# Thirty tiny loads on SyncE's DMA queue, in a decode step of attention beside an MLP

## The chip, the cores and the metric

The kernel runs on one core of a Trainium2 chip. The metric is the device time of one launch in microseconds (us), the median of several runs. Beside the plain runs there is one profiled execution, whose trace gives the times of single instructions and transfers.

## What is computed

```python
x = A_x                                   # 8 tokens (one for each sequence), 640 features
xn = layernorm(x)
q = (xn @ wq) -> 32 heads of 128          # per sequence
p = softmax(q . k_cache * 128**-0.5)      # k_cache, v_cache: [8, 32, 4096, 128], bf16
A = (p . v_cache -> 4096 features) @ wo   # wo: [4096, 640]
B = gelu(layernorm(xn) @ w1 + b1) @ w2 + b2   # 640 -> 1728 -> 640
out = x + A + B                           # [8, 1, 640] bf16
```

The K and V caches are 268 MB each; all the weights together are 15 MB. Each cache element is used once, with one query.

## The kernel before

**Tiles.** The 256 pairs of sequence and head are cut into 32 tiles of one sequence and eight heads. A K tile or a V tile is 8 MiB: 128 partitions (eight heads by 16 parts of the keys), each with 256 keys of 128 bf16 numbers, so 64 KB from one contiguous run of HBM for each partition. SBUF has three slots of that size: KA and KB take the K tiles in turn, VS takes every V tile. Outside the cache loop the same slots hold the weights: wq, q and w1 in VS, w2, b1, b2, x and small scratch in KB, wo in KA.

**Work on a tile.** `dve_chunk` (L701) lets VectorE multiply 176 of the 256 keys of each partition by the query, add and reduce, in two chunks; the other 80 are transposed on TensorE, copied by ScalarE and multiplied on TensorE (`scores`, L680). `act_exp` (L745) turns the tile's scores into probabilities, and `pe_PV` (L765) multiplies them with the V tile in 256 matmuls.

**Loads.** All large loads go out on SyncE's queue in one order. A load is made by the helpers `load` (L419), `load_w2` (L426), `load_k` (L432), `load_v` (L443), `load_wl` (L457) and `load_wn` (L465). Each records a `dma_start` and, ahead of it, the waits on what must be free: a K tile waits until VectorE is done with the K tile two before (the first one in KB waits for `pe_acc0`, L619), a V tile until the PV before has read VS. x and b1 go out on ScalarE's queue.

**The order.** Nothing runs while the helpers are called. `at(pos, fn, ...)` (L416) puts a call in a list, which is sorted by `pos` (L977); each engine records its calls, and the records are played at the end, SyncE's by one plain replay (L980). All instructions are issued by one line of the replay helper, which is why the profile gives line 218 for nearly everything. On SyncE the order before the cache loop is w1, w2 in two pieces, b2 (position -879), wq (-878, L893), the first K tile (-870, L894). Tile i has its work at about 100 i, so the last tile's V stands at 3150. V_CUT (L305) cuts that last V tile into three pieces of 4096, 2816 and 1280 KB. wo is loaded in five pieces: two ahead of the last V tile (2560 and 1280 KB, by WL_CUT) and three behind it (640, 480 and 160 KB, by WN_CUT = (24, 28, 31, 32), positions 3251 to 3253, L953).

**The end.** `fin_wn` (L844) multiplies each of the last three pieces of wo as it arrives into the accumulator that holds x, B and the other heads; `fin_store` (L854) copies, transposes and stores the result. SyncE's last act is to wait for that store.

Of the kernel before, what the change touches and what calls it, by code (L numbers as in the profile page):

```python
# [235 lines left out]
def _replay_pe(e, calls, head, mid, end, late, parity):  # L236

    n = len(head) - 1
    scores = [calls[a:b] for a, b in zip(head[:-1], mid)]
    values = [calls[a:b] for a, b in zip(mid[1:], head[2:] + [end])]  # L240
    assert mid[0] == head[1] and n & (n - 1) == 0

    def special(e, call, r):
        if call[0] != "wait_ge":
            return False
        for k, x in enumerate(parity):
            if x is call[1][0]:
                e.wait_ge(x, ((r + 2 - k) >> 1) * 16 + k)
                return True
        for x in late:  # L250
            if x is call[1][0]:
                e.wait_ge(x, ((r + n - 1) >> n.bit_length()) * 16 + 1)
                return True
        return False

    _replay(e, calls[:head[0]])
    with e.bass.Fori(0, n + 2, engines=OrderedEngineSet([e.engine])) as r:
        reg = e.to_reg(r)
        with e.If_ne(reg, 1):
            _play(e, values, r, 2, special)  # L260
        with e.If_lt(reg, n):
            _play(e, scores, r, 0, special)
        with e.If_eq(reg, n):
            _replay(e, calls[head[n]:mid[n]])
    _replay(e, calls[end:])


def bass_parallel_sum__gqa_block_cached__mixer_channel_mlp__decode_kernel(
# [32 lines left out]
    SLOT = NKEY * DH  # L301
    KA, KB, VS = 0, 1, 2
# [12 lines left out]
    def kslot(i):  # L315
        return KA if i % 2 == 0 else KB
# [4 lines left out]
    with ExitStack() as es:  # L321
        sb = lambda name, shape, dt: es.enter_context(nc.sbuf_tensor(name, shape, dt))
        ps = lambda name, shape, dt: es.enter_context(nc.psum_tensor(name, shape, dt))
        sem = lambda name: es.enter_context(nc.semaphore(name))
# [5 lines left out]
        def part(slot, lo, n, rows=P):  # L330
            return S_sb[0:rows, slot, lo:lo + n]
# [10 lines left out]
        def scratch(n, rows=P):  # L342
            ap = part(KB, o_[0], n, rows)
            o_[0] += n + n % 2
            return ap
# [11 lines left out]
        hT_sb = scratch(NF * B).rearrange("p (c b) -> p c b", b=B)  # L357
        iota_i = scratch(2 * P).bitcast(I32)
        ones_sb = scratch(B, 1)
        assert o_[0] <= SLOT  # L360

        KT_sb = sb("KT_sb", [P, 2, TPB, P], BF)
# [42 lines left out]
        pe, dve, act, sp, pool = (_Eng(sem(f"{n}_s")) for n in ("pe", "dve", "act", "sp", "pool"))  # L405
        pe2, act2 = _Eng(sem("pe2_s")), _Eng(sem("act2_s"))
        ld_s = [_Dma(sem(f"ld_s{s}")) for s in range(3)]
        ld_x, ld_b1, ld_b2, ld_wq, ld_w1, ld_w2, st_o = (
            _Dma(sem(n)) for n in ("ld_x", "ld_b1", "ld_b2", "ld_wq", "ld_w1", "ld_w2", "st_o"))
        ld_vl = [_Dma(sem(f"ld_vl{q}")) for q in range(1, len(V_CUT) - 1)]  # L410
        ld_wl = [_Dma(sem(f"ld_wl{q}")) for q in range(len(WL_CUT) - 1)]
        ld_wn = [_Dma(sem(f"ld_wn{q}")) for q in range(len(WN_CUT) - 1)]
        tk = {}
        prog = []

        def at(pos, fn, *a):  # L416
            prog.append((pos, len(prog), fn, a))
# [4 lines left out]
        def cache_src(cache, i):  # L422
            hq, b = divmod(i, B)
            return cache[b, hq * HS:(hq + 1) * HS].rearrange("h (p j) d -> (h p) j d", j=NKEY)
# [7 lines left out]
        def load_k(i):  # L432
            s = kslot(i)
            if i >= 2:
                sp.wait(tk[("km", i - 2)])
            elif s == KB:
                sp.wait(tk["acc"])
                ld_s[s].n += 1
            tk[("k", i)] = ld_s[s].sig(sp.dma_start(tile[s], cache_src(A_k_cache, i)))
            tk[("kk", i)] = [(ld_s[x].sem, (i + 2 - x) // 2 * 16 + x) for x in (KA, KB)]  # L440
            assert tk[("k", i)] == tk[("kk", i)][s]
# [23 lines left out]
        def load_wn(q):  # L465
            lo, hi = WN_CUT[q], WN_CUT[q + 1]
            tk[("wn", q)] = ld_wn[q].sig(sp.dma_start(
                woN_sb[:, lo - NL * HS:hi - NL * HS, :],
                A_wo[lo * DH:hi * DH, :].rearrange("(h p) n -> p h n", p=P)))

        def consts_pool():
            tk["iota"] = pool.sig(pool.iota(iota_i, [[1, P]], base=0, channel_multiplier=-1))
            for ap, v, d, k in (
                    (w2_sb[:, FR * D:], 0.0, ld_s[KB], 1), (ones_sb, 1.0, ld_vl[0], 1), (eps_sb[:, :], LN_EPS, ld_vl[1], 1),
                    (ini_sb[:, :], 0.0, ld_s[VS], 48), (rs_sb[:, :], 1.0, None, 0)):
                inst = pool.memset(ap, v)
                if d is not None:
                    inst.call[3] = (d.sem, k)
            assert len(ld_vl) == 2
            tk["consts"] = pool.sig(pool.memset(ones_f[:, :], 1.0))  # L480
# [409 lines left out]
        at(-879, load, "b2", ld_b2, b2_sb, B_b2.rearrange("(o f) -> o f", o=1))  # L890
        at(-890, load, "w1", ld_w1, w1_sb, B_w1.rearrange("(p c) f -> p c f", c=DC))
        at(-880, load_w2)
        at(-878, load, "wq", ld_wq, wq_sb, A_wq.rearrange("(p c) n -> p c n", c=DC))  # L893
        at(-870, load_k, 0)  # L894
        at(-800, consts_pool)
        at(-795, idents)
# [22 lines left out]
        for i in range(NQ):  # L919
            o = i * Q  # L920
            last = i == NQ - 1
            if i:
                at(o - 51, load_k, i)
            at(o + 50, load_v, i)
            at(o + 45, qrep, i + 1)
            at(o + 46, pe_qbc, i + 1)
            at(o + 46, act_qbc, i + 1)
            at(o, scores, i)
            at(o + 2, dve_chunk, i, 0)
            at(o + 52, dve_sel, i, 0)  # L930
            at(o + 55, dve_sel, i, 1)
            at(o + 58, dve_chunk, i, 1)
            at(o + 84, dve_max, i)
            at(o + Q + 45, act_exp, i)
            at(o + Q + 48, pe_RS, i)
            at(o + Q + 57, dve_rinv, i)
            at(o + Q + 50, pe_PV, i)
            if not last:
                at(o + Q + 71, act_O, i)
            at(o + Q + 75, o_norm, i)  # L940
# [7 lines left out]
        o = NQ * Q  # L948
        for q in range(len(WL_CUT) - 1):
            at(o - 55 + 0.1 * q, load_wl, q)  # L950
            at(o + 10 + q, fin_wl, q)
        for q in range(len(WN_CUT) - 1):
            at(o + 51 + q, load_wn, q)  # L953
            at(o + 80 + q, fin_wn, q)
# [28 lines left out]
        with nc.allow_low_precision(reason="each sum to bf16 has one bf16 term that is not masked to zero"):  # L983
            _replay_loop(nc.vector, dve.calls, marks["dve"])
        _replay_pe(nc.tensor, pe.calls, head, mid, end[0], [d.sem for d in ld_vl],
                   [ld_s[KA].sem, ld_s[KB].sem])
        nc.sync.wait_ge(*tk["out"])


# [26 lines left out]
```

## Time and profile before

| | us |
|---|---|
| median of 3 runs | 1282.88 (1282.83 to 1282.95) |
| the profiled execution | 1284.83 |
| its span, from the first instruction to the last | 1283.0 |

Of the span PE (TensorE) is busy 54%, VectorE 85%, ScalarE 37%, GpSimd 6%.

How to read the lines. A row of a timeline is: start in us from the span's start, length in us, engine (a q behind the name: the engine's instruction queue issues it), line, operation, output<-input, how often, and in brackets the engine's idle time ahead of it with what ended it. A row of the chain of waits is start, length, what. A row by window is: stretch, its length, then busy time and count of PE, PEld (weight loads), DVE (VectorE), ACT (ScalarE) and POOL (GpSimd), the granted TensorE clock, the busy share of the 16 DMA engines, and GB/s. A row of DMA issues ends in KB and us from issue to the landing of the last part; a row of one tensor gives the issue's shortest, median and longest length in ns, and the first and last start. A row of the queues gives packets, MB and share of 16 engines' time.

### The profile page before, as it was taken

How to read it: one execution, taken by the hardware profiler on the slowest of the kernel's cores; microseconds unless marked ns; L12 is line 12 of the kernel's file. 1: busy time of each engine (PE TensorE's matmuls, PEld its weight loads, DVE VectorE, ACT ScalarE, POOL GpSimd, SP SyncE). 2: the span in 40 equal slices, each digit the busy share in tenths (PEclk: the TensorE clock that was granted, in tenths of full speed). 3: DMA queues.
4: the chain of work that ended last, by engine and by line, in shares of the span. 5: the costliest groups of instructions: out<-in, count | busy, mean ns of one | idle time of the engine just before them, and what ended most of it. 6: DMA issues, size and time to landing. Idle time of an engine off the chain costs nothing.

```text
span 1283.0 us, 34713 instructions
## 1 busy us (share of the span) xinstructions
PE 697.1 (54%) x14014; PEld 581.1 (45%) x14014; DVE 1084.8 (85%) x574; ACT 474.2 (37%) x913; POOL 79.7 (6%) x79
## 2 busy tenths in 40 slices
PE   6856544564544664544664544654545654545655
PEld 2545443453443553433553434543434543434545
DVE  1699998988888988888988888988889988889884
ACT  2254322444322444323444223444223444223441
POOL 2013110000000000000000000000000000000001
PEclk8666555556555665656566656566556656555655
DMA  9999999999999999999999999999999999999998
GB/s 400 450 420 409 425 445 437 425 425 450 433 425 425 456 427 425 425 458 425 425 425 456 427 425 431 450 427 425 441 441 425 425 445 437 425 425 454 429 413 372
DMA packets 11584, 551.93 MB, mean 430 GB/s; under 512 B 1261, under 2 KB 2358, under 8 KB 2359
## 3 DMA queue, kind: packets, MB, share of 16 engines
q1 hardware_dynamic: 11506, 551.79, 99.6%
q8 instruction: 6, 0.10, 0.0%
q10 hardware_dynamic: 68, 0.02, 0.0%
q14 instruction: 4, 0.02, 0.0%
HBM read 551.80 MB, written 0.01 MB: 430 GB/s over the span
## 4 chain that ended last, share of the span: by engine, by line
DMA 76%; PE 21%; DVE 1%; issue 1%; POOL 0%; ACT 0%; SPq 0%; DVEq 0%; POOLq 0%
DMA S_sb<-in_A_v_cache_dram 71%; PE PV_ps L218 17%; PE TR_ps L218 2%; DMA S_sb<-in_A_k_cache_dram 2%; DMA S_sb<-in_A_wo_dram 2%; PE S_ps L218 1%; DMA S_sb<-in_B_w_dram 1%; DVE S_sb L218 1%; POOL qrep_sb L218 0%; PE QB_ps L218 0%; DVE ini_sb L218 0%; ACT KT_sb L218 0%; PE CH_ps L218 0%; PE ACC_ps L218 0%; SPq L218 0%
## 5 line engine op out<-in xcount | busy, mean ns | idle before, releaser
L218 PE MATMUL TR_ps<-ident_bf,S_sb 128*128 128x128 bf16 (+1 forms) x2570 | 340.2, 270 | 386.6 <-DMA S_sb<-in_A_k_cache_dram 358.7
L218 ACT ACTIVATE KT_sb<-TR_ps 128x1024 bf16<-128x1024 bf16 x320 | 327.6, 1024 | 459.2 <-PE TR_ps L218 447.3
L218 DVE TENSOR_TENSOR S_sb<-S_sb,qbc_sb 128x14976 bf16<-128x14976 bf16 x64 | 383.9, 5999 | 130.8 <-DMA S_sb<-in_A_k_cache_dram 129.5
L218 PEld LDWEIGHTS TR_ps<-ident_bf,S_sb 128*128 (+1 forms) x2570 | 243.6, 101 | 444.1 <-issue 387.5
L218 DVE TENSOR_REDUCE ini_sb<-S_sb 128x117 f32<-128x7488 bf16 x64 | 385.3, 6020 | 2.2
L218 PE MATMUL PV_ps<-P_sb,S_sb 128*128 128x8 bf16 x8448 | 231.3, 175 | 41.8 <-DMA S_sb<-in_A_v_cache_dram 39.3
L218 PEld LDWEIGHTS PV_ps<-P_sb,S_sb 128*128 128x128 bf16 x8448 | 228.8, 103 | 44.8 <-DMA S_sb<-in_A_v_cache_dram 42.1
L218 DVE TENSOR_TENSOR S_sb<-S_sb 128x7488 bf16<-128x7488 bf16 x64 | 197.9, 3091 | 2.2
L218 PE MATMUL S_ps<-qrep_sb,KT_sb 128*128 128x8 bf16 x2560 | 121.7, 177 | 29.8 <-ACT KT_sb L218 25.1
L218 ACT ACTIVATE P_sb<-ini_sb 128x256 bf16 (+1 forms) x256 | 126.0, 496 | 7.4 <-DVE ini_sb L218 7.4
L218 PEld LDWEIGHTS S_ps<-qrep_sb,KT_sb 128*128 128x128 bf16 x2560 | 90.9, 101 | 58.6 <-ACT KT_sb L218 40.6
L218 ACT ACTIVATE oU_sb<-PV_ps 128x8 f32<-128x8 f32 x32 | 5.7, 178 | 287.2 <-PE PV_ps L218 253.9
L218 POOL TENSOR_TENSOR oT_sb<-oU_sb,ri_sb 128x8 bf16<-128x8 f32 x31 | 52.1, 1680 | 391.9 <-ACT oU_sb L218 391.9
L218 POOL COPY qrep_sb<-qT_sb 128x128 bf16<-128x128 bf16 x33 | 19.0, 576 | 781.6 <-PE S_ps L218 751.2
L218 PE MATMUL CH_ps<-rs_sb,ones_f 128*128 128x8 f32 x66 | 19.5, 369 | 87.1 <-ACT P_sb L218 85.1
L218 PEld LDWEIGHTS CH_ps<-rs_sb,ones_f 128*128 128x128 f32 x66 | 16.5, 311 | 92.4 <-issue 92.4
L218 ACT ACTIVATION_READ_ACCUMULATOR P_sb<-ini_sb 128x1 f32 x256 | 48.5, 189 | 0.0
L218 DVE TENSOR_TENSOR S_ps<-S_ps,mask_sb 128x512 f32<-128x512 f32 (+1 forms) x65 | 32.5, 500 | 1.5 <-PE S_ps L218 1.5
L218 DVE TENSOR_REDUCE ini_sb<-S_ps 128x64 f32<-128x512 f32 x64 | 31.4, 491 | 2.2
L218 PE MATMUL QB_ps<-ident_bf,qrep_sb 128*128 128x128 bf16 x33 | 8.8, 268 | 23.5 <-POOL qrep_sb L218 23.1
L218 PEld LDWEIGHTS QB_ps<-ident_bf,qrep_sb 128*128 128x128 bf16 x33 | 3.3, 101 | 26.7 <-POOL qrep_sb L218 26.2
L218 DVE TENSOR_REDUCE ini_sb<-ini_sb 128x1 f32<-128x256 f32 x32 | 13.4, 420 | 1.1
(75 smaller groups left out, 135.3 us busy)
## 6 DMA issues: line engine op xcount, KB each, us to landing
S_sb<-in_A_wq_dram SPq DMA_DIRECT2D x1, 5120.0 KB, 24.0
S_sb<-in_A_v_cache_dram SPq DMA_DIRECT2D x1, 4096.0 KB, 15.3
S_sb<-in_A_v_cache_dram SPq DMA_DIRECT2D x1, 2816.0 KB, 18.6
S_sb<-in_A_wo_dram SPq DMA_DIRECT2D x1, 2560.0 KB, 31.8
S_sb<-in_B_w_dram SPq DMA_DIRECT2D x1, 2160.0 KB, 9.1
S_sb<-in_B_w_dram SPq DMA_DIRECT2D x1, 2080.0 KB, 12.1
S_sb<-in_A_wo_dram SPq DMA_DIRECT2D x1, 1280.0 KB, 34.5
S_sb<-in_A_v_cache_dram SPq DMA_DIRECT2D x1, 1280.0 KB, 21.3
```

What stands on the lines that cost most here:

```text
L218: inst = getattr(e, name)(*out, **kw)
```

## The change

A new helper, `ladder`, issues fifteen DMAs on SyncE's queue. The k-th of them, for k from 1 to 15, reads k runs of two bf16 numbers (4 bytes), 128 bytes apart, from b1 in HBM, and writes them into a scratch row of partition 0. Nothing reads them. They share one semaphore. The helper is called twice: at position -878.5, between b2 and wq, and at 3250.9, between the last piece of the last V tile and the first of the three last pieces of wo. The second K tile, whose slot holds the first scratch row, waits for the first fifteen loads; SyncE waits for all thirty before its wait for the store.

```diff
+        lad_sb = [ap.rearrange("o (j k e) -> o j k e", j=16, k=16) for ap in (
+            scratch(16 * 16 * 4, 1), part(KA, SLOT - 1024, 1024, 1))]
...
+        ld_t = _Dma(sem("ld_t"))
...
             elif s == KB:
-                sp.wait(tk["acc"])
+                sp.wait(tk["acc"], tk["lad"])
                 ld_s[s].n += 1
...
+        def ladder(row, src):
+            for k in range(1, 16):
+                tk["lad"] = ld_t.sig(sp.dma_start(
+                    lad_sb[row][:, k, 0:k, 0:2], src[0:k * 64].rearrange("(o k e) -> o k e", o=1, k=k)[:, :, 0:2]))
...
         at(-880, load_w2)
+        at(-878.5, ladder, 0, B_b1)
         at(-878, load, "wq", ld_wq, wq_sb, A_wq.rearrange("(p c) n -> p c n", c=DC))
...
+        at(o + 50.9, ladder, 1, B_b1)
         for q in range(len(WN_CUT) - 1):
             at(o + 51 + q, load_wn, q)
...
+        nc.sync.wait_ge(*tk["lad"])
         nc.sync.wait_ge(*tk["out"])
```

## The prediction

> **What bounds the kernel now.** I read the page first: its slices, the queues, and the shares of the chain that ended last.
>
> ```profile
> span 1283.0 us, 34713 instructions
> DMA  9999999999999999999999999999999999999998
> DMA packets 11584, 551.93 MB, mean 430 GB/s; under 512 B 1261, under 2 KB 2358, under 8 KB 2359
> DMA 76%; PE 21%; DVE 1%; issue 1%; POOL 0%; ACT 0%; SPq 0%; DVEq 0%; POOLq 0%
> ```
>
> The 16 DMA engines are busy in every slice, and three quarters of the chain is DMA. Next I read busy time by window, to see whether the stream itself or a hole in it sets the length.
>
> ```profile
> 0.00:25.60 25.60, 15.34 (x68) 5.51 (x69) 5.11 (x17) 6.88 (x11) 6.72 (x13) 0.89 1.00 417
> 45.10:84.30 39.20, 26.22 (x467) 21.51 (x463) 35.29 (x18) 15.31 (x17) 0.34 (x2) 0.54 0.98 422
> 84.30:103.80 19.50, 13.64 (x344) 11.97 (x342) 19.40 (x5) 9.74 (x23) 3.70 (x1) 0.68 0.93 401
> 250.00:589.00 339.00, 176.37 (x3515) 149.29 (x3515) 292.08 (x147) 130.33 (x251) 15.04 (x18) 0.58 1.00 433
> 650.00:1240.00 590.00, 315.15 (x6412) 267.38 (x6412) 511.68 (x257) 225.74 (x429) 26.66 (x30) 0.57 1.00 434
> ```
>
> The last two columns are the share of the DMA engines and GB/s. From 250 us on the share is 1.00 at 433 to 434 GB/s, which is 27.1 GB/s for each of 16 engines: there is no hole to fill. The one hole is at 84 to 104 us: 7% of 19.5 us is 1.4 us. It ends with a V tile issued late, so what sets that issue matters. The chain of waits, SyncE's timeline and VectorE's timeline answer that and show the end.
>
> ```profile
> 80.48 24.66 DMA S_sb<-in_A_k_cache_dram
> 103.35 0.33 SPq L218 DMA_DIRECT2D S_sb<-in_A_v_cache_dram  x1
> 46.63 7.96 DVE L218 TENSOR_TENSOR S_sb<-S_sb,qbc_sb 128x14976 bf16<-128x14976 bf16 x1 [3.88 <-DMA S_sb<-in_A_k_cache_dram]
> 1256.49 23.51 DMA S_sb<-in_A_wo_dram
> 1280.05 0.71 PE ACC_ps L218 x20
> ```
>
> VectorE idles 3.88 us for the first K tile and starts at 46.63; its work on that tile, then exp and the first PV, lead to the V tile's issue at 103.35, while the K tile ahead of it in the stream lands at 80.48 + 24.66 = 105.14. So whatever delays the first K tile's landing delays that V issue equally, and all after it, since the stream does not idle again. At the far end the last wo pieces land at 1280.0 and the short tail follows. The change can cost at two places only: **before wq**, by way of the first K tile, and **before the last wo pieces**.
>
> **What the change does.** Each ladder is fifteen DMAs of 1 to 15 rows of 4 bytes: 120 rows, 480 bytes. The two add 30 issues on SyncE. Nothing is removed; wq and the first K tile move behind the first ladder, the last three pieces of wo behind the second (the loop over WN_CUT makes three, not four). A wait on the tiny loads is put in front of the second K tile and one before the end.
>
> **Step 1, issue time at the start.** Rows for one issue and for what hides it:
>
> ```profile
> 2.54 0.48 SPq L218 DMA_DIRECT2D S_sb<-in_B_b_dram  x1
> 3.07 0.43 SPq L218 DMA_DIRECT2D S_sb<-in_A_wq_dram  x1
> 0.73 0.60 ACTq L218 DMA_DIRECT2D S_sb<-in_A_x_dram  x1
> 2.74 0.88 DVE L218 BATCH_NORM_STATS2 S_sb<-S_sb 8x6 f32<-8x320 bf16 x2 [0.25 <-DMA S_sb<-in_A_x_dram]
> L218 SPq DMA_DIRECT2D S_sb<-in_B_w_dram x3: 390/417/834, 0.7 to 1.7; - x3
> S_sb<-in_B_w_dram SPq DMA_DIRECT2D x1, 80.0 KB, 13.3
> S_sb<-in_A_wq_dram SPq DMA_DIRECT2D x1, 5120.0 KB, 24.0
> ```
>
> The nearest row to a tiny load is b2, one row on the same queue: from 2.54 to the next issue at 3.07 it takes 0.53 us. Fifteen take 8.0 us, so wq is issued at 11.1 instead of 3.07. The bounds are the cheapest SyncE issue shown (0.33, with 0.05 between two: 0.38, hence 5.7 us) and the dearest plain one (x, 0.60 + 0.05, hence 9.8 us). The cover: the last piece of w2 was issued at 1.7 and landed 13.3 us later, at 15.0; wq landed at 27.1; the 12.1 us between, for 5.24 MB, is 433 GB/s, so wq's data follow directly behind w2's. x went from issue at 0.73 to its reader at 2.74 in 2.0 us. So wq's data arrive unbroken if it is issued by 15.0 - 2.0 = 13.0. That leaves 9.9 us, or 0.66 us for each tiny load. At 0.53 it holds with 1.9 us to spare, and even at the upper bound. **Cost taken: 0.** Were the cover gone, each us beyond 9.9 would delay wq and the first K tile, which is queued right behind wq, by a us. The second K tile is issued near 30 us, after the tiny loads have landed: its new wait costs nothing.
>
> **Step 2, the tiny rows inside the stream.**
>
> ```profile
> q10 hardware_dynamic: 18, 0.01, 0.4%
> S_sb<-in_A_wo_dram SPq DMA_DIRECT2D x1, 640.0 KB, 22.7
> S_sb<-in_A_wo_dram SPq DMA_DIRECT2D x1, 480.0 KB, 23.5
> S_sb<-in_A_wo_dram SPq DMA_DIRECT2D x1, 160.0 KB, 23.4
> 1257.04 11.16 SPq L218 DMA_DIRECT2D S_sb<-in_A_wo_dram  x1
> ```
>
> The first row is ScalarE's queue in the first 28 us: 18 packets for x and b1. x has 8 rows and b1 one; with one completion packet for each row that is 18. So I let a load of n rows use n engines, and the busiest engine gets 15 rows and 15 completions, the sixteenth none. The 160 KB piece has 8 rows of 1280 bytes for each engine and was issued 0.55 us after the 480 KB one (1257.04 against 1256.49), landing 23.4 against 23.5 us after its issue: 0.45 us later by these rounded figures. With its completion that is 0.05 us a packet, and 1280 bytes at 27.1 GB/s are already 0.047. A packet's overhead is thus a few ns. Bounds for 30 packets: 0 and 30 x 0.05 = 1.5 us; I take 0.01 us each, an estimate near the low end because the nearest row leaves next to nothing beyond its bytes: 0.3 us on the busiest engine, once per ladder. The end sees it only if that engine is also the one that lands last, which no view shows; I take a third of it each time: **+0.1 at the start, +0.1 at the end.**
>
> The Trainium skill, DMA: Bandwidth & Descriptors, section Why a DMA increments its semaphore by 16 and not by 1, says that such a load runs on the lowest-numbered k engines, k dividing the slowest dimension; the 18 packets agree, and by it the ladder would skew the engines in order, the first most.
>
> **Step 3, issue time at the end.**
>
> ```profile
> 1256.01 12.19 SPq L218 DMA_DIRECT2D S_sb<-in_A_wo_dram  x3
> S_sb<-in_A_v_cache_dram SPq DMA_DIRECT2D x1, 4096.0 KB, 15.3
> S_sb<-in_A_v_cache_dram SPq DMA_DIRECT2D x1, 2816.0 KB, 18.6
> S_sb<-in_A_v_cache_dram SPq DMA_DIRECT2D x1, 1280.0 KB, 21.3
> 1251.76 4.22 SPq L218 DMA_DIRECT2D S_sb<-in_A_v_cache_dram  x3
> ```
>
> Fifteen issues of 0.53 move the first of the three pieces from 1256.0 to 1264.0; its data are due when the last V piece has landed, about 1277 (issued by 1255.98, the end of the three V issues, 21.3 later at most). That is covered by 10 us. But the queue has a limit: the issue at 1257.04 hung for 11.16 us, until 1268.2, about 1 us after the first V piece had landed (1251.8 + 15.3 = 1267.1). At that moment there stood ahead of it, for each engine, 8 + 8 rows of V and 32 + 24 of wo, 72; so the limit is near 72 to 80 rows (an estimate from these sizes). With up to 30 small packets more on one engine, the 480 KB and 160 KB pieces find room only as the last V piece drains, near 1277. Issued then, at 0.5 us each, the last lands some 2 us later at 1279.5, and it was due at 1280.4. **Cost taken: 0**, with 0.9 us of margin.
>
> The sum: 0 + 0.1 + 0.1 + 0 = **+0.2 us**. The profiled execution took 1284.83 us, 1.8 of it outside the span of 1283.0, and becomes 1285.0. The median of the runs, 1282.88, is 1.95 below that execution; the same +0.2 makes it **1283.1**.
>
> **Rivals.**
>
> *A, the issues are dearer than their cover (slower).* A load of 1 to 15 rows may take SyncE longer than one of 128. It decides from 0.66 us each, and costs 15 times what is above: at 0.80 us 2.1, at 1.0 us 5.1 us (1288.0). For it: x, with 8 rows, took 0.60. Against it: that was ScalarE's first, and b2 took 0.48. Chance 0.09.
>
> *B, the full queue makes the last pieces late (small loss).* If each of the last two issues goes through only after the piece before has begun to drain, at 1278.7 instead of 1277, the last lands at 1281.1, +0.7; if each waits for the one before to land, 2.0 us twice less the margin and what overlaps, about +2.6. For it: the 11.16 us. Against: the limit is freed by V rows, which drain earlier. 0.7 to 2.6 us: 1283.8 to 1285.7. Chance 0.10.
>
> *C, each tiny load pays its latency in the stream (much slower).* 15 x 2.0 us, twice, is 60 us at most, 1343. Against it: three loads issued 0.45 us apart at the start streamed at full rate, and 1261 packets under 512 B already pass at a share of 1.00. Chance 0.02. [...]
>
> *D, the skew helps (faster).* If engines out of step held 433 GB/s where they now have less, there is to gain: 417 against 433 over 25.6 us is 0.95 us, 422 over 39.2 is 1.0, and the hole 1.4: at most 3.4 (1279.5). Against it: the stretch from 650 us runs at the engines' own 27.1 GB/s, and the hole comes from the late issue, which skew does not move. Chance 0.07, of which 0.03 beyond 0.2%.
>
> *E, the change does other than it says.* If the tiny loads left some other way, no time would change: inside the forecast's range. Chance 0.02.
>
> **Chances.** Forecast 0.70, its own range 1282.6 to 1283.8. About 0.2%, or 2.6 us, is what a measurement of this kernel can tell from no change. Faster by over that: 0.05 (D's upper part 0.03, and 0.02 set aside from the forecast for what no view shows). Slower by over that: 0.13 (A 0.07, C 0.02, B 0.02, and 0.02 set aside in the same way). Within it: the rest, 0.82. The range leaves out the top of A, C and the best of D: 1281.4 to 1286.2.
>
> **What would show it.** SyncE's timeline: fifteen issues from 3.07, wq issued near 11.1 and below 13.0, and wq still landing at 27.1; VectorE's first long multiply still at 46.6; a V issue at 103.4. At the end: the first wo piece issued near 1264, a long hang of a later issue that ends by 1277.5, the last piece landing at 1280.5. Wrong would be: wq landing after 27.5 (A or C), the last wo piece landing over 2 us behind the last V piece's due time (B), or a first K tile before 46 us (D).

## The result, and the profile after

The changed kernel takes 1286.00 us, the median of 14 runs (1285.70 to 1286.44); the kernel before took 1282.95 in the 14 runs beside it. That is 3.05 us more, a ratio of 1.0023 (95% interval 1.0015 to 1.0030). The forecast was 1283.1, with 1282.6 to 1283.8 as its own range. The time is 2.9 us above that forecast. It lies 0.2 us inside the upper end of the wide range, 1286.2, and at 0.24% it is past the 0.2% within which the prediction saw it with a chance of 0.82.

Every run also has its span, from the first instruction to the last. The medians are (the spans of the kernel before come from its runs beside the experiments below):

| | time, us | span, us | outside the span, us |
|---|---|---|---|
| kernel before | 1282.9 | 1281.1 | 1.83 |
| changed kernel | 1286.0 | 1284.7 | 1.30 |

So inside the span the change costs **3.6 us**; 0.5 us less lies outside it. The ends of the span stand where they stood: in both kernels SyncE's first load goes out 0.73 to 0.74 us after the start, and the last transpose begins about 1.9 us ahead of the end. The profiled execution of the kernel before, with its 1283.0, was one of the few that take about 1.9 us longer than the median, which matters below.

The page of the changed kernel gives its span and packets; the rows by window show the DMA share in the column before the last:

```profile
span 1285.0 us, 34744 instructions
DMA packets 12064, 551.94 MB, mean 430 GB/s; under 512 B 1740, under 2 KB 2837, under 8 KB 2838
```
```profile
0.00:25.60 25.60, 15.16 (x67) 5.34 (x68) 5.07 (x17) 6.88 (x11) 6.72 (x13) 0.93 0.88 351
84.30:103.80 19.50, 11.37 (x312) 10.23 (x311) 19.43 (x3) 7.78 (x21) 3.31 (x1) 0.66 1.01 434
650.00:1240.00 590.00, 314.83 (x6407) 267.08 (x6406) 511.70 (x257) 224.94 (x428) 26.68 (x30) 0.58 1.00 433
```

There are 480 packets more, 240 for each ladder, which fits its 120 rows with one completion each. The first 25.6 us have lost 12% of their DMA share, 3.1 us: a hole, part of which is made up in the next 19.5 us (share 1.06 against 0.99). The hole at 84 to 104 us, which the prediction read in the kernel before, is not here, and the long middle runs at 433 GB/s, nearly as before (434).

SyncE's timeline shows what made the hole, the row of b1 and b2 gives the length of one issue (shortest, median, longest in ns), the DMA issues give the landing, and VectorE's row shows the consequence:

```profile
2.28 11.35 SPq L218 DMA_DIRECT2D S_sb<-in_B_b_dram  x16
13.67 0.56 SPq L218 DMA_DIRECT2D S_sb<-in_A_wq_dram  x1
```
```profile
L218 SPq DMA_DIRECT2D S_sb<-in_B_b_dram x31: 288/702/777, 2.3 to 1267.0; - x31
```
```profile
S_sb<-in_A_wq_dram SPq DMA_DIRECT2D x1, 5120.0 KB, 15.6
S_sb<-in_B_w_dram SPq DMA_DIRECT2D x1, 80.0 KB, 13.7
```
```profile
49.67 7.96 DVE L218 TENSOR_TENSOR S_sb<-S_sb,qbc_sb 128x14976 bf16<-128x14976 bf16 x1 [8.79 <-DMA S_sb<-in_A_k_cache_dram]
```

b2 and the fifteen tiny loads keep SyncE from 2.28 to 13.63. The median issue takes 0.70 us, not b2's 0.48. wq is issued at 13.67 instead of 3.07 and lands at 29.3 instead of 27.1, although the last piece of w2 landed at 15.4, nearly as before (15.0). VectorE starts the first K tile at 49.67 instead of 46.63.

The hole is seen best between 12.5 and 14.5 us, first in a second profile of the kernel before (experiment e3 below), then in the changed kernel:

```profile
12.50:14.50 2.00, 2.00 (x7) 0.42 (x5) 0.00 (x0) 0.18 (x2) 0.00 (x0) 1.00 1.17 497
12.50:14.50 2.00, 2.00 (x6) 0.46 (x4) 0.00 (x0) 0.51 (x1) 0.00 (x0) 1.00 0.24 64
```

64 GB/s instead of 497: nearly all of w2 has been moved by 12.5 us, 2.9 us before its last part lands, and wq's first data come only after 14.5.

At the end, TensorE's rows show when the last V piece (x40) and the pieces of wo (x20) had landed. In the changed kernel, and then in a profile of the kernel before that is typical of its median (experiment e3 below):

```profile
1277.96 1.24 PE L218 MATMUL PV_ps<-P_sb,S_sb 128*128 128x8 bf16 x40 [0.57 <-DMA S_sb<-in_A_v_cache_dram]
1280.87 0.70 PE L218 MATMUL ACC_ps<-oT_sb,S_sb 128*128 128x8 bf16 x20 [1.67 <-DMA S_sb<-in_A_wo_dram]
```
```profile
1275.48 1.23 PE L218 MATMUL PV_ps<-P_sb,S_sb 128*128 128x8 bf16 x40 [0.66 <-DMA S_sb<-in_A_v_cache_dram]
1277.26 0.69 PE L218 MATMUL ACC_ps<-oT_sb,S_sb 128*128 128x8 bf16 x20 [0.55 <-DMA S_sb<-in_A_wo_dram]
```

From the last V piece to the first piece of wo it is now 2.91 us, and was 1.78: the second ladder costs 1.1 us there. The V piece itself is 2.48 us later, which the start has cost: with the first ladder alone (e1) it is 2.47 us later, at 1277.95.

### The profile page after: what moved, and what is told of

It is laid out like the page before. It is cut to its first block, busy times and chain, and to the rows that moved or that the text cites. A ratio compares the mean times of both kernels' runs of the same rounds, so it can differ in the third digit from the quotient of the medians.

```text
span 1285.0 us, 34744 instructions
## 1 busy us (share of the span) xinstructions
PE 694.7 (54%) x14014; PEld 580.0 (45%) x14014; DVE 1084.8 (84%) x574; ACT 474.3 (37%) x913; POOL 79.0 (6%) x79
## 4 chain that ended last, share of the span: by engine, by line
DMA 77%; PE 17%; DVE 2%; SPq 2%; issue 1%; POOL 0%; ACT 0%; DVEq 0%; POOLq 0%
DMA S_sb<-in_A_v_cache_dram 71%; PE PV_ps L218 16%; DMA S_sb<-in_A_k_cache_dram 5%; SPq L218 2%; DVE S_sb L218 1%; DMA S_sb<-in_A_wo_dram 1%; PE TR_ps L218 1%; POOL qrep_sb L218 0%; DVE ini_sb L218 0%; PE S_ps L218 0%; ACT KT_sb L218 0%; DVE S_ps L218 0%; POOL S_sb L218 0%; PE ACC_ps L218 0%; PE QB_ps L218 0%
## 5 line engine op out<-in xcount | busy, mean ns | idle before, releaser
L218 ACT ACTIVATION_READ_ACCUMULATOR P_sb<-ini_sb 128x1 f32 x256 | 48.5, 189 | 0.0
L218 DVE TENSOR_REDUCE ini_sb<-ini_sb 128x1 f32<-128x256 f32 x32 | 13.4, 420 | 1.1
## 6 DMA issues: line engine op xcount, KB each, us to landing
S_sb<-in_A_wo_dram SPq DMA_DIRECT2D x1, 2560.0 KB, 31.8
```

The lines of the kernel that those rows point to most:

```text
L218: inst = getattr(e, name)(*out, **kw)
```

## The experiments

Theory 1: the fifteen issues hold SyncE so long that the stream runs dry ahead of wq. Theory 2: the tiny packets cost in the stream, wherever they stand. Theory 3: the whole loss is at the end. Each kernel was timed beside the kernel before, on the same chip; "span" is the median of the runs' spans, against 1281.1 (1281.0 for e12) of the kernel before.

| kernel | time, us | ratio (95% interval) | span against before, us |
|---|---|---|---|
| e1 first ladder alone | 1284.99 | 1.0017 (1.0008 to 1.0026) | +2.6 |
| e2 second ladder alone | 1283.68 | 1.0006 (0.9997 to 1.0015) | +1.2 |
| e3 kernel before | 1282.93 | 0.9999 (0.9990 to 1.0008) | 0.0 |
| e4 first ladder behind the first K tile | 1287.83 | 1.0039 (1.0025 to 1.0052) | +5.4 |
| e5 the same without the wait | 1283.42 | 1.0006 (0.9997 to 1.0015) | +1.0 |
| e6 first ladder, twelve loads | 1283.15 | 1.0002 (0.9993 to 1.0011) | +0.7 |
| e7 first ladder, 16 rows each | 1284.60 | 1.0013 (1.0004 to 1.0022) | +2.2 |
| e8 second ladder behind wo | 1283.90 | 1.0008 (0.9999 to 1.0017) | +1.5 |
| e9 first ladder behind wq | 1283.59 | 1.0004 (0.9995 to 1.0013) | +1.2 |
| e10 second ladder ahead of V | 1283.53 | 1.0003 (0.9994 to 1.0012) | +1.1 |
| e11 second ladder, one row each | 1282.80 | 1.0000 (0.9991 to 1.0009) | +0.4 |
| e12 second ladder, 16 rows each | 1284.60 | 1.0014 (1.0005 to 1.0023) | +2.3 |

Eight intervals of ratios include 1; beside them stand the spans, which within one kernel mostly agree to 0.3 us, so a difference of 0.4 is hardly clear of zero. In every kernel with tiny loads 1.29 to 1.34 us lie outside the span, against 1.82 to 1.84 in the kernel before. The expectations counted in time and so missed these 0.5 us; the readings below use spans.

**e1, the first ladder alone.**

```diff
-        at(o + 50.9, ladder, 1, B_b1)
```


> The first ladder alone. Theory 1 (issue time): fifteen tiny issues take SyncE 10.9 us, wq's data come some 1.9 us after the stream has run dry, and the rest of the kernel moves with it: 1284.9, +2.0. Theory 2 (tiny packets in the stream): the loss is made where the tiny packets run, by stalls behind them, alike at both places: about half of the +3.05, 1284.4. Theory 3 (the end alone): the delay at the start is absorbed by the compute chain behind the first K tile, and the whole loss is at the end: 1283.0.

Measured 1284.99, as theory 1 has it; theory 3 is out. SyncE's timeline and the window of its profile:

```profile
13.57 0.56 SPq L218 DMA_DIRECT2D S_sb<-in_A_wq_dram  x1
```
```profile
0.00:25.60 25.60, 15.62 (x70) 5.83 (x71) 4.93 (x17) 6.87 (x11) 6.72 (x13) 0.87 0.88 353
```

The hole of 12% is there with the first ladder alone.

**e2, the second ladder alone.**

```diff
-        at(-878.5, ladder, 0, B_b1)
-                sp.wait(tk["acc"], tk["lad"])
+                sp.wait(tk["acc"])
```


> The second ladder alone. Theory 1: the first wo row behind the tiny packets is late by about 1 us on some engines, +1.1, 1284.0, with the last V piece landing as in the kernel before. Theory 2: about half of the +3.05, 1284.4. Theory 3: 1286.0.

Measured 1283.68, +0.77 in time and +1.2 in the span. TensorE's rows show the place:

```profile
1275.00 1.24 PE L218 MATMUL PV_ps<-P_sb,S_sb 128*128 128x8 bf16 x40 [0.58 <-DMA S_sb<-in_A_v_cache_dram]
1278.03 0.69 PE L218 MATMUL ACC_ps<-oT_sb,S_sb 128*128 128x8 bf16 x20 [1.79 <-DMA S_sb<-in_A_wo_dram]
```

3.03 us from the last V piece to wo, 1.25 more than in e3: the size that theory 1 gave, though for this place theory 1 too had blamed the row behind the tiny packets and not the issues. The two ladders alone, 2.6 and 1.2, add up to 3.8 against 3.6 together.

**e3, the kernel before, once more.**

> The kernel before, unchanged, profiled once more: 1282.9 by every theory. Its first profiled execution took 1284.83, 1.95 above its median, and shows a hole in the stream at 104 us. If that hole belongs to that one execution, this profile has a DMA share near 1.00 between 84 and 104 us and a span near 1281; if it belongs to the kernel, the share is 0.93 again and the span is 1283.0.

Measured 1282.93, and a profile with a span of 1281.3. Its window, SyncE's issue of the V tile, and TensorE's row ahead of the second tile, and below them the same row of TensorE from the first profile of the kernel before:

```profile
84.30:103.80 19.50, 11.39 (x312) 10.32 (x311) 19.40 (x5) 7.62 (x21) 1.86 (x1) 0.50 1.01 434
99.89 0.33 SPq L218 DMA_DIRECT2D S_sb<-in_A_v_cache_dram  x1
75.15 1.13 PE L218 MATMUL TR_ps<-ident_bf,S_sb 128*128 128x128 bf16 x7 [5.01 <-DVE S_sb L218]
```
```profile
77.54 0.63 PE L218 MATMUL TR_ps<-ident_bf,S_sb 128*128 128x128 bf16 x3 [7.44 <-issue]
```

The hole at 84 to 104 us belonged to that first profiled execution. In it TensorE idled 7.44 us without a wait that the profile shows, in e3 only 5.01, and the V tile was issued at 103.35, 3.5 us later than in e3. Why TensorE started late was not tried. In the typical execution the V issue at 99.89 has room: the K tile issued at 80.5 is still landing.

**e4, the first ladder behind the first K tile.**

```diff
-        at(-878.5, ladder, 0, B_b1)
+        at(-869, ladder, 0, B_b1)
-        at(o + 50.9, ladder, 1, B_b1)
```


> The first ladder alone, moved behind the first K tile's load, so that SyncE issues wq and that tile as early as before, while the same tiny packets still run in the stream, between the first and the second K tile. Theory 1: the loss of the first ladder is gone, 1283.0, at most +0.3. Theory 2: the packets cost the same wherever they run: as much as the first ladder ahead of wq, 1284.4. Theory 3: 1283.0.

Measured 1287.83, which no theory expected. SyncE's timeline, and its waits:

```profile
4.34 10.77 SPq L218 DMA_DIRECT2D S_sb<-in_B_b_dram  x15
48.56 0.35 SPq L218 DMA_DIRECT2D S_sb<-in_A_k_cache_dram  x1
```
```profile
SPq L203 <- DMA S_sb<-in_B_b_dram: 33.4, 1, 33.4
```

The edit made a new wait bite. The second K tile takes the slot that holds the scratch row, so it waits for the tiny loads; these now stand behind the first K tile's 8 MiB in the queue and land only after it. The second K tile was issued at 48.56 instead of near 30, with nothing else queued. The run tells nothing of issue time; it was a confounded edit, and e5 mends it.

**e5, the same without the wait.** The tiny loads get their own 480 values in SBUF.

```diff
+        lad_sb = sb("lad_sb", [1, 120, 4], BF)
-                sp.wait(tk["acc"], tk["lad"])
+                sp.wait(tk["acc"])
-                    lad_sb[row][:, k, 0:k, 0:2], ...
+                    lad_sb[:, k * (k - 1) // 2:k * (k + 1) // 2, 0:2], ...
+        at(-869, ladder, 0, B_b1)
```


> The first ladder alone, behind the first K tile's load as in e4, but into 480 values of its own in SBUF, so that the second K tile's load need not wait for it. Theory 1 (issue time ahead of wq, and in e4 the added wait): the packets themselves cost next to nothing, 1282.9 to 1283.3, and the second K tile is issued near 30 us again. Theory 2 (tiny packets in the stream cost wherever they run): 1284.5 to 1285.

Measured 1283.42, +0.50, and +1.0 in the span: more than "next to nothing", and far from e1's 2.6. So theory 2 is not wrong but partial: the packets cost about 1 us in the stream, and the place ahead of wq costs more than that.

**e6, twelve loads.**

```diff
-            for k in range(1, 16):
+            for k in range(1, 13):
```


> The first ladder alone, cut to twelve loads of 1 to 12 rows. With fifteen, wq was issued at 13.57 and 2.08 us were lost, so under theory 1 the issue is in time until about 11.5. Twelve loads take 8.5 us and wq is issued near 11.2: nothing is lost, 1282.9 to 1283.1. Theory 2: twelve fifteenths of 2.08, 1284.6.

Measured 1283.15, +0.7 in the span.

```profile
2.28 9.01 SPq L218 DMA_DIRECT2D S_sb<-in_B_b_dram  x13
11.33 0.52 SPq L218 DMA_DIRECT2D S_sb<-in_A_wq_dram  x1
```

With wq issued at 11.33 the loss is no more than what the packets cost in e5. Three loads more, wq at 13.57, cost another 1.9 us. Their 42 rows account for some 0.4 of it (an estimate, from e5's 1.0 for 120 rows); the rest says that the cover ends between the two, as theory 1 has it.

**e7, sixteen rows each.**

```diff
-                    lad_sb[row][:, k, 0:k, 0:2], src[0:k * 64]...
+                    lad_sb[row][:, k, 0:16, 0:2], src[0:16 * 64]...
```


> The first ladder alone, each of its fifteen loads with 16 rows of 4 bytes, on every engine alike. Under theory 1 all depends on the price of one issue. If it grows with the rows as in the ladder (0.67 us at 2 rows, 0.78 at 15), wq is issued near 15.4 and some 3.9 us are lost, 1286.8. If what is dear is a number of rows that does not fill all 16 engines, an issue takes 0.33 to 0.43 as with 128 rows, wq is issued near 10 and nothing is lost, 1282.9. Theory 2, with twice the packets: above 1285.

Measured 1284.60, between the two guesses, as is the price of an issue: SyncE needs 10.17 us for sixteen (with b2), about 0.63 each.

```profile
2.28 10.17 SPq L218 DMA_DIRECT2D S_sb<-in_B_b_dram  x16
12.49 0.58 SPq L218 DMA_DIRECT2D S_sb<-in_A_wq_dram  x1
```

Its +2.2 in the span is what the same packets cost in e12 (+2.3), where no hole is possible; within the 0.3 us nothing is left for wq's lateness here.

**e8, the second ladder behind wo.**

```diff
-        at(o + 50.9, ladder, 1, B_b1)
+        at(o + 53.5, ladder, 1, B_b1)
```


> The second ladder alone, behind the last piece of wo instead of ahead of the last three. If the 0.77 us of e2 are a stall of the wo rows behind the tiny packets, they are gone: 1282.9. If they come from the issues on SyncE or from the number of packets in the queue, they stay: 1283.7 or more, since the issues now end near 1277 and the last wait of SyncE may come late.

Measured 1283.90: the loss changes its cause. SyncE's timeline, and its waits:

```profile
1266.68 14.86 SPq L218 DMA_DIRECT2D S_sb<-in_B_b_dram  x15
```
```profile
SPq L997 <- DMA S_sb<-in_B_b_dram: 1.3, 1, 1.3
```

The three issues of wo take 12.15 us, nearly as in the kernel before (12.18 in e3). The tiny ones behind them begin only at 1266.68 and end at 1281.54; SyncE then waits 1.3 us for the tiny loads at the very end, and that wait is the loss. The rows of wo themselves are free of any stall, as TensorE's rows show:

```profile
1275.52 1.24 PE L218 MATMUL PV_ps<-P_sb,S_sb 128*128 128x8 bf16 x40 [0.71 <-DMA S_sb<-in_A_v_cache_dram]
1277.19 0.70 PE L218 MATMUL ACC_ps<-oT_sb,S_sb 128*128 128x8 bf16 x20 [0.43 <-DMA S_sb<-in_A_wo_dram]
```

From the last V piece to wo it is 1.67 us, against 1.78 in e3 and 3.03 in e2. So e2's loss needs the tiny rows ahead of wo.

**e9, the first ladder one place later.**

```diff
-        at(-878.5, ladder, 0, B_b1)
+        at(-877, ladder, 0, B_b1)
-        at(o + 50.9, ladder, 1, B_b1)
```


> The first ladder alone, one place later: behind wq's load and ahead of the first K tile's, so wq is issued near 2.9 and SyncE has until about 23.5 for the first K tile. Theory 1 (issue time ahead of wq): the hole is gone, 1282.9, plus what the tiny packets cost in the stream, 0.5 as in e5, so 1283.4. Theory 2 (packets alone): 1285.0, as in e1.

Measured 1283.59, +1.2 in the span against e1's +2.6. SyncE's timeline and the first window:

```profile
2.89 0.64 SPq L218 DMA_DIRECT2D S_sb<-in_A_wq_dram  x1
3.57 10.76 SPq L218 DMA_DIRECT2D S_sb<-in_B_b_dram  x15
```
```profile
0.00:25.60 25.60, 14.37 (x87) 6.56 (x87) 5.74 (x18) 6.87 (x11) 6.72 (x13) 1.00 1.03 417
```

The same loads with the same issue time (10.76 us), and no hole, because 5 MiB of wq are in the queue meanwhile. The difference to e1, 1.4 us, is the price of SyncE's lateness; the other 1.2 us are the packets', as far as the two simply add. So the time of e1 met theory 1's +2.0 partly by luck: the theory had no packets in it, and their 1.2 us are offset in part by the 0.5 us saved outside the span.

**e10, the second ladder ahead of the last V tile**, with the buffer of e5.

```diff
-        at(o + 50.9, ladder, 1, B_b1)
+        at(o - 50.1, ladder, 1, B_b1)
```


> The second ladder alone, issued in SyncE's idle time ahead of the last V tile, with a buffer of its own; its packets run ahead of rows of 32 KB instead of rows of 1280 bytes. If the rows behind tiny packets stall wherever these stand, the loss is 0.5 to 0.8 as in e5 and e2: 1283.4 to 1283.7. If the stall needs the short rows of wo, it is gone: 1282.9.

Measured 1283.53, +1.1 in the span. SyncE had nothing else to issue there, and it issues the last pieces of wo from 1254.30, as early as in e3 (1254.49), so no late issue is in this loss. The packets cost the same ahead of rows of 32 KB as ahead of rows of 1280 bytes.

**e11, one row each.**

```diff
-                    lad_sb[row][:, k, 0:k, 0:2], src[0:k * 64]...
+                    lad_sb[row][:, k, 0:1, 0:2], src[0:64]...
```


> The second ladder alone, fifteen loads of one row each: 15 rows in place of 120, all on one engine if a load of one row runs on one. If the busiest engine alone sets the loss, it stays at 0.77: 1283.7. If the loss is made on all engines that carry tiny rows, or in the order of the engines, it falls to a small part: 1283.0.

Measured 1282.80, no change in time, +0.4 in the span. An issue of one row is cheap:

```profile
1254.17 4.72 SPq L218 DMA_DIRECT2D S_sb<-in_B_b_dram  x15
```

Fifteen take 4.72 us, 0.31 each with the gap behind it. The loss falls to a third of e2's; from the last V piece to wo it is 2.50 us, 0.72 more than in e3, but the V piece is 0.36 us earlier. That fits two readings: the tiny rows cost little on one engine, or they cost much on an engine that is not the last to land. e12 tells these apart.

**e12, sixteen rows each at the end**, the edit of e7 on the second ladder.

> The second ladder alone, each of its fifteen loads with 16 rows, so that every engine gets fifteen tiny rows, the one that lands last among them. If the loss is made on each engine that carries tiny rows, and e11 was free only because its one engine was not the last, the loss is 0.8 or more: 1283.7 to 1284.2. If the loss of e2 came from the unequal shares of the ladder, it is gone: 1282.9 to 1283.1.

Measured 1284.60, +2.3 in the span.

```profile
1275.14 1.24 PE L218 MATMUL PV_ps<-P_sb,S_sb 128*128 128x8 bf16 x40 [0.57 <-DMA S_sb<-in_A_v_cache_dram]
1278.99 0.69 PE L218 MATMUL ACC_ps<-oT_sb,S_sb 128*128 128x8 bf16 x20 [2.62 <-DMA S_sb<-in_A_wo_dram]
```

From the last V piece to wo it is 3.85 us, 2.07 more than in e3. SyncE issued wo earlier than in e2 (from 1264.01 against 1265.34), so what counts is the rows and not the time of the issue. The stream over the same 2.5 us, in e3 and then here:

```profile
1273.50:1276.00 2.50, 1.84 (x69) 1.75 (x67) 0.00 (x0) 0.00 (x0) 0.00 (x0) 0.50 1.02 365
1273.50:1276.00 2.50, 1.93 (x72) 1.84 (x69) 0.00 (x0) 0.00 (x0) 0.00 (x0) 0.50 0.92 152
```

The engines count as busy, yet move less than half. The trace also holds the length of every single packet, which no view prints, and there the loss can be found. A tiny row or its completion takes 0.009 us. In e12, 16 rows of wo, as many as there are engines, take 1.21 to 1.59 us each, and 32 more take 0.09 to 0.63; in e3 no row of wo takes over 0.07. So it is the rows behind the tiny ones that are held up. Over the usual 0.055 us they take 31.8 us more in all, 2.0 for each of 16 engines. The same count gives 13.4 us in e2 (0.84 for each engine), 2.0 us in e11 (0.13, most of it in one row of 1.37 us), and in e10 11.8 us on 18 rows of the last V tile (0.74); in e1 15 rows of wq are longer, by 11.0 us in all, and in e9 ten rows of the first K tile, by 11.6, so the packets cost both of these kernels about the same.

That is 0.09 to 0.13 us for each tiny row with its completion. The losses in the span (2.3, 1.2, 0.4 and 1.1 us for e12, e2, e11 and e10) follow the mean over the engines, with some 0.3 us more each time, which these rows do not explain. So the second reading of e11 is right: the one row of 1.37 us points to one engine that carried all fifteen loads, and it was held up as long as the engines of e12, but the stream as a whole lost little by it. How the engines even this out is not shown.

## Why the prediction was right or wrong

**What bounds the kernel** was right: the stream of loads, at 433 GB/s in both kernels. That the change can cost at two places only, ahead of wq and ahead of the last wo pieces, held.

**The hole at 84 to 104 us** was read from one execution and taken for the kernel. e3 shows that the typical execution has none. It did not enter the sum, but it was part of rival D's price, and the argument that a late first K tile is passed on by way of the late V issue was the wrong path: in the changed kernel VectorE starts that tile 3 us later, but the V tile is issued at 100.72, only 0.8 us later than in e3. The delay is passed on directly: a stream that runs dry once and is full ever after ends that much later.

**Step 1** failed, and cost 1.4 of the 3.6 us in the span. It priced an issue by b2, one row, at 0.53 us and took x, 0.65, for the upper bound. The tiny loads took 10.8 us in all, 0.72 each, outside that bound. b2 was a poor stand-in: e11's loads of one row take 0.31 each, even less than b2, and loads of 2 to 15 rows more than twice that. The rival had this right: A's point of decision was 0.66 us each, and 0.72 lies past it. A's price was too small: 15 x 0.72 - 9.9 gives 0.9 us, and the comparison of e1 with e9 gives 1.4. So the cover was mis-sized too. It was counted to the last landing of w2, at 15.0, but the changed kernel moved only 64 GB/s from 12.5 to 14.5 us: most of the engines were done with w2 by then. The sign that the prediction itself had named, wq landing after 27.5, came: 29.3.

**Step 2** failed in size, and is the larger part of the miss: 2.2 to 2.4 of the 3.6 us. It took 0.01 us for a packet and 0.1 us at each place, with 1.5 us for the busiest engine as the upper bound. The runs show 1.0 to 1.2 us at each place, and 2.1 to 2.3 with fifteen rows on every engine, beyond the bound. The argument was that a row of 1280 bytes takes hardly longer than its bytes, so a packet has next to no cost of its own. That was right as far as it went: a tiny packet takes 0.009 us. It left out what a run of tiny rows does to the row behind it, which e12's trace shows: 1.21 to 1.59 us instead of 0.055. The third that was taken for the unequal shares should have been about a half (1.2 of 2.3 us, e2 against e12). How the stall comes about inside an engine is not shown.

**Step 3** held: the late issue at the end costs nothing that these runs show. The second ladder's issues, 10.76 us, end at 1267.8, and wo's data were due ten us later; e10, which issues wo as early as the kernel before, loses as much as e2. The feared hang was short: the three wo issues took 6.95 us together, against 12.19 before.

```profile
1257.06 10.76 SPq L218 DMA_DIRECT2D S_sb<-in_B_b_dram  x15
1267.86 6.95 SPq L218 DMA_DIRECT2D S_sb<-in_A_wo_dram  x3
```

Rival B did not come, though 160 KB landed late for the reason of step 2. Rival C, 2 us for each tiny load, is excluded: fifteen cost 2.3 us at the most. Rival D gained nothing: the ladder that gives the engines unequal shares costs less than equal shares (e2 against e12), but more than no ladder.

**The sum**, corrected: 1.4 for SyncE's lateness, 1.2 for the first ladder's packets, 1.2 for the second's, less 0.2 by which the two ladders alone exceed both together: 3.6 in the span. The 0.2 is a remainder, within the 0.3 us by which spans differ, and no term of its own. Outside the span 0.5 us are saved, which no step foresaw: 3.1 in time.

**Luck.** That the time lies inside the stated range is owed to the width of the range, which took in most of A and B, and to the 0.5 us saved outside the span. The forecast itself said +0.2 with no cost for the issues, and the loss that came had been given a chance of 0.13.

## What to carry to other kernels

Price an added DMA by a load of the same form, not of the same size: here one of 2 to 15 short rows held its queue for 0.6 to 0.8 us, most of those with 128 long rows for 0.33. Do not price a tiny packet by its own length alone: the row behind it paid. Where one queue feeds a stream that must not run dry, count how many us of data are queued ahead when the extra issues begin, and put them behind the large load rather than ahead of it; but then no later load may wait for them, since they land after it. And profile an execution twice before a hole in it is made part of an argument.

## What was not expected of the hardware

- An issue on SyncE took 0.22 to 0.29 us for one row of 4 bytes in e11, 0.62 to 0.78 for the ladder's loads of 2 to 15 rows (e1), a median of 0.59 for 16 rows (e12), and 0.33 for nearly all K and V tiles of 128 rows; wq, also 128 rows, took 0.43 to 0.77. Whether the form of the rows or the number of engines makes the difference was not separated.
- A tiny packet took 0.009 us, but a tiny row with its completion cost its stream 0.09 to 0.13 us (e1, e2, e9 to e12): rows of 1280 bytes behind a run of them took up to 1.59 us (e12), where among their like they took 0.055 to 0.058.
- Tiny loads behind an 8 MiB load in the same queue landed only after it: VectorE had that load's tile at 46.6 us, and SyncE waited for the tiny ones until 48.5 (e4).
- With tiny loads in the kernel, 1.3 us lie outside the span instead of 1.83, in all eleven variants (1.29 to 1.34). The cause was not tried; each of them has one more semaphore and one more wait at the end.
